# Decay products of a chunked recurrence: another normalization, and their inverses by a backward scan on VectorE

## The chip, the cores and the metric

The kernel runs on one core of one Trainium2 chip. The time is that of one execution on the device, in microseconds (us), as the median of several runs. The profile is that of one further execution of the same program.

## The reference

Three stages follow one another: a linear recurrence over 768 steps for 4 x 8 heads with a state of 40 x 40, an MLP with a leaky ReLU, and a gated MLP behind a root-mean-square norm. The change is in the first.

```python
def _attn_ref(r, k, v, w, a, b):                      # each (4, 8, 768, 40)
    state = np.zeros((B, H, D, D))
    for t in range(S):
        y[:, :, t] = np.einsum('bhd,bhde->bhe', rt, state)
        Sa = np.einsum('bhde,bhe->bhd', state, at)
        state = state * wt[:, :, None, :] - np.einsum('bhd,bhe->bhde', Sa, bt)
        state = state + np.einsum('bhd,bhe->bhde', vt, kt)
...
x = attn_out.transpose(0, 2, 1, 3).reshape(B * S, H * D)   # 3072 x 320
h = x @ w_in; x = np.maximum(0.01 * h, h) @ w_out          # d_ff 2048
xn = x / rms(x) * rms_g
out = (silu(xn @ w_gate) * (xn @ w_val)) @ w_out2          # d_ff 1536
```

The decays `w` lie between 0.85 and 0.95.

## The kernel before

The recurrence is computed in chunks of C = 32 steps, NCH = 24 of them. A chunk has two units (`u = 2c + hs`), each with two batches on the partitions (rows 0 to 39 and 64 to 103 hold the 40 channels) and 8 heads along the free axis, so there are NU = 48 units. Within a chunk the decays enter as running products over time; they are folded into `a`, `k` and `b`, so that the chunk becomes matrix products and a triangular system.

`prep(u)` does this folding, in nine steps that the plan places separately. `scan` (L165): VectorE forms the running products P of one chunk by one `tensor_tensor_scan` over all 8 heads, and the reciprocal of the last product. `ratio` (L170): GpSimd copies the last product (`pc`) and divides all others by it (`pp`). `suffix` (L174): five GpSimd products of shifted slices double the length of products towards the chunk's end, 1, 2, 4, 8, 16, in place in the tile `raw`; they end up as `q`. `ai` (L181) multiplies `a` with `pp`, `kq` (L184) multiplies `k` and `b` with `q` into `kb`, both on GpSimd. `end` (L187): ScalarE squares `pp` and `q` and sums them into `ok`, which a later check reads, and SyncE starts the load of `raw` for the unit after next. For units 0 and 2 (`FAST`) VectorE does GpSimd's part.

Behind it: `stageA` multiplies `kb` with `AI` on TensorE; VectorE masks the result (L238) and ScalarE copies it; over DRAM it is laid out anew for `solve`, in which VectorE solves the triangular systems of a chunk in 31 steps (`tt`, L278, L281 and L283, all with both inputs in SBUF). Stages T, B, C, E and F carry the state through TensorE, with ScalarE and VectorE between them. In `stageF` VectorE makes the next state (`state`, L392, multiplied by `pc` of the following chunk) and the output (`out`, L398, multiplied by `pp`), each with one input in PSUM.

The first MLP runs in between. Its input products (L602) go through ScalarE (L654, L655), VectorE (L654) and GpSimd, which makes the low part `gl` (L655); then come its output products `o` (L610 to L613). Weights are converted and split as jobs `w` (L466 to L480) on VectorE, ScalarE and GpSimd. The second MLP follows when the recurrence is done.

The order is written out by hand: each engine runs its queue in the order in which the program issues. `PROLOG` lists the steps of the first units one by one. From then on each chunk has 12 slots, and `PLAN` gives for even and odd chunks (and some by number) the slot of each step of `prep` for the units three chunks ahead, of the solve's steps, and of the loads and stores. For even chunks the nine steps of the first unit stand in slots 0, 2, 3, 3, 5, 5, 5, 5, 8 and those of the second in 6, 7, 10, 10, 10, 10, 10, 10, 11; for odd chunks in 0, 1, 1, 1, 2, 4, 6, 6, 8 and in 5, 7, 7, 9, 10, 10, 10, 10, 10.

Of the kernel before, what the change touches and what calls it, by code (L numbers as in the profile page):

```python
# [9 lines left out]
F32 = mybir.dt.float32  # L10
# [4 lines left out]
ACTF = mybir.ActivationFunctionType  # L15
ALU = mybir.AluOpType
# [5 lines left out]
C = 32  # L22
NCH = S // C
NU = 2 * NCH
RW = 8 * 34 + 3 * 8 * 32
CW = 32 + 32 + 40 + 32
NT = B * S
DM, DF1, DF2 = 320, 2048, 1536
# [52 lines left out]
class Attn:  # L81
# [3 lines left out]
    def __init__(self, ctx, tc, raw, rT, vS, vT, cst, xs, ok):  # L85
        nc = self.nc = tc.nc
        self.tc = tc
        self.raw_d, self.rT_d, self.vS_d, self.vT_d, self.xs = raw, rT, vS, vT, xs
        per = self.per = ctx.enter_context(tc.tile_pool(name="a_per", bufs=1))
        self.p2 = ctx.enter_context(tc.tile_pool(name="a_p2", bufs=2))  # L90
        self.dr = ctx.enter_context(tc.tile_pool(name="a_dr", bufs=2, space=DRAM))
        self.psp = ctx.enter_context(tc.tile_pool(name="a_ps", bufs=2, space=PSUM))
        self.ends = []
        self.fill = 0
        self.rawt, self.PP, self.PC, self.KBt, self.Nsc, self.Tsc = {}, {}, {}, {}, {}, {}
        self.NT, self.TT, self.tm, self.RHS = {}, {}, {}, {}
        self.load(0)
        self.cst = per.tile([128, CW - 32], F32, name="cst")
        nc.sync.dma_start(out=self.cst, in_=cst[:, 0:CW - 32])
        self.load(1)  # L100
        c = self.cst
        self.mA, self.mE, self.id40 = c[:, 0:32], c[:, 32:64], c[:, 64:104]
        self.d1 = per.tile([128, 272], BF16, name="d1")
        nc.gpsimd.memset(self.d1, 0.0)
        nc.gpsimd.memset(self.d1[:, 0:272:34], 1.0)
        self.ok = ok
        self.AI = per.tile([128, 2, 8, 72], F32, name="ai")
        self.VU = per.tile([128, 2, 8, 64], F32, name="vu")
        self.XZ = per.tile([128, 2, 2, 8, 72], F32, name="xz")
        self.RB = per.tile([128, 2, 2, 8, 40], F32, name="rb")  # L110
        self.G = [per.tile([128, 2, 2, 8, 40], F32, name=f"g{i}") for i in range(3)]
        self.Xa = [per.tile([128, 2, 2, 8, 32], F32, name=f"xa{i}") for i in range(3)]
# [30 lines left out]
    def load(self, u):  # L143
        t = self.p2.tile([128, RW], F32, tag="raw", name="raw")
        self.nc.sync.dma_start(out=t[0:104], in_=self.raw_d[u // 2, u % 2])
        self.rawt[u] = t

    def prep(self, u, fast=False):


        nc = self.nc
        eng = nc.vector if fast else nc.gpsimd
        c, hs = u // 2, u % 2
        raw = self.rawt.pop(u)
        w = raw[0:104, 0:272].rearrange("p (h t) -> p h t", t=34)
        k, b, a = (raw[0:104, 272 + 256 * j:528 + 256 * j].rearrange("p (h t) -> p h t", t=32) for j in range(3))
        q = w[:, :, 2:34]
        P = self.p2.tile([128, 8, 34], F32, tag="P", name="P", bufs=1)
        rp = self.p2.tile([128, 8], F32, tag="rp", name="rp")
        pc = self.p2.tile([128, 8], F32, tag="pc", name="pc", bufs=8)  # L160
        pp = self.p2.tile([128, 8, 32], F32, tag="pp", name="pp", bufs=8)
        kb = self.p2.tile([128, 8, 64], F32, tag="kb", name="kb")
        self.PP[u], self.PC[u], self.KBt[u] = pp, pc, kb

        def scan():  # L165
            nc.vector.tensor_tensor_scan(out=P[0:104].rearrange("p h t -> p (h t)"), data0=raw[0:104, 0:272],  # L166
                                         data1=self.d1[0:104], initial=0.0, op0=ALU.mult, op1=ALU.add)
            nc.vector.reciprocal(rp[0:104], P[0:104, :, 32])

        def ratio():  # L170
            eng.tensor_copy(pc[0:104], P[0:104, :, 32])
            eng.tensor_tensor(pp[0:104], P[0:104, :, 0:32], rp[0:104, :, None].to_broadcast([104, 8, 32]), op=ALU.mult)

        def suffix(*ds):  # L174
            for d in ds:
                eng.tensor_tensor(q[:, :, 0:32 - d], q[:, :, 0:32 - d], q[:, :, d:32], op=ALU.mult)  # L176

        def square(i, x):
            nc.scalar.activation(k, x, ACTF.Square, accum_out=self.ok[0:104, 2 * u + i:2 * u + i + 1])

        def ai():  # L181
            eng.tensor_tensor(self.AI[0:104, hs, :, 0:32], a, pp[0:104], op=ALU.mult)

        def kq(x, o):  # L184
            eng.tensor_tensor(kb[0:104, :, o:o + 32], x, q, op=ALU.mult)

        def end():  # L187
            square(0, pp[0:104])
            square(1, q)
            if u + 2 < NU:  # L190
                self.load(u + 2)

        self.ends.append(end)
        return [scan, ratio, lambda: suffix(1, 2), lambda: suffix(4, 8), lambda: suffix(16), ai,
                lambda: kq(k, 0), lambda: kq(b, 32), end]

    def check(self, flag):

# [172 lines left out]
    def stageF(self, u):  # L371
        nc = self.nc
        c, hs = u // 2, u % 2
        xz, g, rb = self.XZ, self.G[c % 3], self.RB
        last = c == NCH - 1
        n = 32 if last else 72
        ps = self.ps("psF")
        for h in range(8):
            for p in range(2):
                f0, f1 = FR[p]  # L380
                k0, k1 = KF[p]
                nc.tensor.matmul(ps[f0:f1, h // 4, 72 * (h % 4):72 * (h % 4) + n], g[k0:k1, p, hs, h, :], xz[k0:k1, p, hs, h, 0:n],
                                 start=True, stop=True)
        psv = ps[:, :, 0:288].rearrange("p a (h x) -> p a h x", x=72)
        y = self.p2.tile([128, 8, 32], F32, tag="y", name="y")
        pp = self.PP.pop(u)
        self.PC.pop(u)

        def state(p):
            f0, f1 = FR[p]  # L390
            pc = self.PC[u + 2]
            nc.vector.tensor_tensor(rb[f0:f1, p, hs].rearrange("p (a h) d -> p a h d", a=2), psv[f0:f1, :, :, 32:72],  # L392
                                    pc[f0:f1].rearrange("p (a h) -> p a h", a=2)[:, :, :, None].to_broadcast([40, 2, 4, 40]),
                                    op=ALU.mult)

        def out(p):
            f0, f1 = FR[p]
            nc.vector.tensor_tensor(y[f0:f1].rearrange("p (a h) t -> p a h t", a=2), psv[f0:f1, :, :, 0:32],  # L398
                                    pp[f0:f1].rearrange("p (a h) t -> p a h t", a=2), op=ALU.mult)
            b = 2 * p + hs  # L400
            nc.sync.dma_start(out=self.xs[c // 2].rearrange("(h e) (b c t) -> c b e h t", e=40, b=4, c=2)[c % 2, b],
                              in_=y[f0:f1])

        return [lambda f=f, p=p: f(p) for f in ([out] if last else [state, out]) for p in range(2)], []

    def stageT(self, u):
# [467 lines left out]
def run(ctx, tc, nc, raw, rT, vS, vT, cst, w_in, w_out, w_gate, w_val, w_out2, rms_g, out, xs, flag):  # L874
# [37 lines left out]
    def at(g, *fs):  # L912
        todo[g][2].extend(fs)
# [17 lines left out]
    def of(c):  # L931
        return PLAN.get(c, PLAN["odd" if c % 2 else "even"])

    def plan(c):

        g = 12 * c
        P = of(c)
        if c + 3 < NCH:
            for h in range(2):
                parts = {}  # L940
                for n, k in enumerate(P["prep"][h]):
                    at(g + k, lambda n=n, h=h, parts=parts: (parts.setdefault(0, A.prep(2 * c + 6 + h) if not parts else None)[n])())
# [213 lines left out]
def _layouts(r, k, v, w, a, b):  # L1156
    def ft(x):
        return x.reshape(2, 2, H, NCH, C, D).transpose(3, 1, 0, 5, 2, 4)

    def pad(x, fill=0.0):  # L1160
        y = np.full(x.shape[:2] + (104,) + x.shape[4:], fill, np.float32)
        for p in range(2):
            y[:, :, 64 * p:64 * p + D] = x[:, :, p]
        return y

    wp = pad(ft(w), 1.0)
    ws = np.concatenate([np.zeros_like(wp[..., :1]), wp, np.ones_like(wp[..., :1])], -1)
    raw = np.concatenate([x.reshape(NCH, 2, 104, -1) for x in (ws, pad(ft(k)), pad(ft(b)), pad(ft(a)))], -1)
    rT = np.ascontiguousarray(ft(r).transpose(0, 2, 3, 1, 4, 5)).reshape(NCH, 2, D, 512)
    vT = np.ascontiguousarray(pad(ft(v)).transpose(0, 2, 1, 3, 4)).reshape(NCH, 104, 512)  # L1170
    vS = np.ascontiguousarray(v.reshape(2, 2, H, NCH, C, D).transpose(3, 0, 4, 1, 2, 5)).reshape(NCH, 2, C, 640)
    return np.ascontiguousarray(raw), rT, vS, vT
# [26 lines left out]
```

## Time and profile before

| what | value |
|---|---|
| median of 3 runs | 1410.51 us (1409.41 to 1413.34) |
| the profiled execution | 1411.78 us, span 1409.8 us |
| busy: TensorE / VectorE / ScalarE / GpSimd | 1214.3 / 1042.2 / 590.2 / 592.3 us |
| mean granted TensorE clock | 0.900 of full speed |

The span runs from the first to the last instruction. In rows of the profile PE is TensorE (PEld its weight loads), DVE VectorE, ACT ScalarE, POOL GpSimd and SP SyncE. An engine's busy time includes time for which an instruction that has begun is held up. "L283" is line 283 of the kernel; a name before "<-" is the tile written, those behind it are read.

### The profile page before, as it was taken

Reading aid. Unit: us, or ns where it says so; the run is one execution under the profiler, and the core shown is the slowest. Engines: PE = TensorE matmul, PEld = TensorE weight load, DVE = VectorE, ACT = ScalarE, POOL = GpSimd, SP = SyncE. Lnnn points to the kernel's source line nnn. Section 1 sums busy time; section 2 is a strip of 40 time slices with the busy share of each in tenths; the row PEclk is TensorE's granted clock in tenths of the full one; section 3 lists DMA queues with packets and bytes.
Section 4 is the critical chain, followed back from the end, with each engine's and each line's share of the span. In section 5 each row is a group of like instructions: output and inputs, shape, how many; then the busy total and the mean of one; then the engine's idle time right before and its main releaser. Section 6 shows DMA issues by size and latency. Waiting matters only on the chain. (4 is left out here: it accounts for less than half of the span.)

```text
span 1409.8 us, 38871 instructions
## 1 busy us (share of the span) xinstructions
PE 1214.3 (86%) x15609; PEld 1122.0 (80%) x15609; DVE 1042.2 (74%) x2757; ACT 590.2 (42%) x1531; POOL 592.3 (42%) x921
## 2 busy tenths in 40 slices
PE   6677579888788787789878888999999999999996
PEld 4565468777777676778767777898999999999996
DVE  7979999999999999999999988845543333333332
ACT  4335664444434443444443444445633333333332
POOL 6546554545454555544455553223222222222221
PEclk8787588889988989898898989999999999999998
DMA  6536456455536364554544443234200000000000
GB/s 154 129 86 138 122 123 138 117 114 112 120 89 123 96 128 101 109 128 96 120 104 95 88 86 66 56 68 121 68 20 20 20 20 20 20 20 20 21 22 18
DMA packets 243925, 116.90 MB, mean 83 GB/s; under 512 B 194712, under 2 KB 223256, under 8 KB 243736
## 3 DMA queue, kind: packets, MB, share of 16 engines
q1 hardware_dynamic: 223224, 86.14, 28.3%
q10 hardware_dynamic: 20512, 28.19, 7.3%
q8 instruction: 125, 2.05, 0.6%
q14 instruction: 64, 0.52, 0.1%
HBM read 86.36 MB, written 23.99 MB: 78 GB/s over the span
## 5 line engine op out<-in xcount | busy, mean ns | idle before, releaser
L655 POOL TENSOR_TENSOR gl<-t,gh 128x512 fp32r<-128x512 f32 x96 | 131.3, 1368 | 275.9 <-ACT gh L655 274.0
L760 POOL TENSOR_TENSOR gl<-s,gh 128x256 fp32r<-128x256 f32 x144 | 106.4, 739 | 296.2 <-issue 163.2
L757 DVE TENSOR_TENSOR s<-psg,s 128x256 f32<-128x256 f32 x144 | 61.1, 424 | 223.2 <-ACT s L756 222.5
L283 DVE TENSOR_TENSOR tt<-tt,tmp 128x60 f32<-128x60 f32 (+19 forms) x548 | 209.4, 382 | 13.7
L281 DVE TENSOR_TENSOR tmp<-tt,nt 128x60 f32<-128x60 f32 (+19 forms) x548 | 175.3, 320 | 14.4
L176 POOL TENSOR_TENSOR raw<-raw 104x248 f32<-104x248 f32 (+4 forms) x230 | 138.9, 604 | 15.8 <-DVE P L166 2.8
L610 PE MATMUL o<-w1oh,gh 128*128 128x320 f32 x384 | 141.8, 375 | 2.2 <-ACT x L673 2.2
L655 ACT CAST gh<-t 128x512 fp32r<-128x512 f32 x96 | 59.5, 619 | 171.3 <-DVE t L654 163.7
L611 PE MATMUL o<-w1ol,gh 128*128 128x320 f32 x384 | 130.3, 345 | 0.0
L231 PE MATMUL psA<-ai,kb 40*64 40x72 f32 x1536 | 75.8, 263 | 60.6 <-DVE tt L283 24.5
L231 PEld LDWEIGHTS psA<-ai,kb 40*64 40x64 f32 x1536 | 67.9, 166 | 70.4 <-issue 38.9
L602 PE MATMUL psh<-xh,w1ih 128*128 128x256 f32 x384 | 123.4, 342 | 0.5 <-DVE t L654 0.5
L759 ACT CAST gh<-s 128x256 fp32r<-128x256 f32 x144 | 58.5, 406 | 139.2 <-DVE s L758 139.2
L278 DVE SCALAR_TENSOR_TENSOR tt<-nt,tt 128x27 f32<-128x27 f32 (+9 forms) x300 | 109.4, 391 | 4.4 <-DMA nt<-nsc 3.2
L756 ACT ACTIVATE s<-psg 128x256 f32<-128x256 f32 x144 | 55.4, 385 | 115.2 <-PE psg L602 113.4
L602 PE MATMUL psh<-xh,w1il 128*128 128x256 f32 x384 | 103.6, 290 | 0.0
L356 PE MATMUL psE<-xz,vu 40*64 40x72 f32 x1536 | 70.7, 252 | 34.5 <-DVE tt L283 32.8
L613 PE MATMUL o<-w1oh,gl 128*128 128x320 f32 x384 | 97.9, 340 | 0.0
L356 PEld LDWEIGHTS psE<-xz,vu 40*64 40x64 f32 x1536 | 63.2, 156 | 42.6 <-issue 22.3
L610 PEld LDWEIGHTS o<-w1oh,gh 128*128 128x128 f32 x384 | 84.9, 221 | 10.5 <-ACT x L673 2.4
L611 PEld LDWEIGHTS o<-w1ol,gh 128*128 128x128 f32 x384 | 85.7, 223 | 0.0
L602 PEld LDWEIGHTS psh<-xh,w1ih 128*128 128x128 f32 x384 | 76.1, 198 | 12.0 <-DVE t L654 0.8
(171 smaller groups left out, 3551.5 us busy)
## 6 DMA issues: line engine op xcount, KB each, us to landing
raw<-in_raw_dram SPq DMA_DIRECT2D x48, 422.5 KB
nt<-nsc SPq DMA_DIRECT2D x96, 128.0 KB
wst<-in_w_out_dram ACTq DMA_DIRECT2D x23, 256.0 KB
vu<-in_vT_dram SPq DMA_DIRECT2D x24, 208.0 KB
wst<-in_w_in_dram ACTq DMA_DIRECT2D x16, 256.0 KB
xa<-ai SPq DMA_DIRECT2D x48, 80.0 KB
rb<-in_vS_dram SPq DMA_DIRECT2D x48, 80.0 KB
xz<-in_rT_dram SPq DMA_DIRECT2D x48, 80.0 KB
```

The costliest lines, as they stand in the source:

```text
L176: eng.tensor_tensor(q[:, :, 0:32 - d], q[:, :, 0:32 - d], q[:, :, d:32], op=ALU.mult)
L231: nc.tensor.matmul(ps[t0:t1, h // 4, 72 * (h % 4):72 * (h % 4) + 72], kb[f0:f1, h, :], self.AI[f0:f1, hs, h, :], start=True, stop=True)
L278: return [lambda j=j: nc.vector.scalar_tensor_tensor(tt[:, j, s + 1:32], nt[:, s, s + 1:32], tt[:, j, s:s + 1], tt[:, j, s + 1:32], op0=AL ...
L281: return [lambda: nc.vector.tensor_tensor(tmp, tt[:, 0:J, s:s + 1].to_broadcast([128, J, L]), nt[:, s:s + 1, s + 1:32].to_broadcast([128, ...
L283: lambda: nc.vector.tensor_tensor(tt[:, 0:J, s + 1:32], tt[:, 0:J, s + 1:32], tmp, op=ALU.add)]
L356: nc.tensor.matmul(ps[t0:t1, h // 4, 72 * (h % 4):72 * (h % 4) + 72], vu[f0:f1, hs, h, :], xz[f0:f1, p, hs, h, :], start=True, stop=True)
L602: self.nc.tensor.matmul(out, a, x, start=i == 0, stop=i == len(ops) - 1)
L610: mm(out[m], gh[:, sl], h[f], start=first, stop=False)
L611: mm(out[m], gh[:, sl], l[f], start=False, stop=False)
L613: mm(out[m], gl[:, sl], h[f], start=False, stop=last)
L655: [lambda: nc.scalar.copy(gh, t), lambda: nc.gpsimd.tensor_tensor(gl, t, gh.bitcast(F32), op=ALU.subtract)])]
L760: nc.gpsimd.tensor_tensor(gl, s, gh.bitcast(F32), op=ALU.subtract)
```

## The change

The products of a chunk are no longer divided by the last of them: P itself (1 at the chunk's beginning) takes the place of `pp`, and its last column that of `pc`. In place of the suffix products `q` the tile R holds the inverses 1/P. They come from a second `tensor_tensor_scan`, which runs backward over the same decays and in place in `raw`, started in each head by the reciprocal of the head's last product, which the first scan's step puts into a tile `dR` of zeros. So `ratio` becomes `back` on VectorE, the three steps of `suffix` are empty, and the two products for `kb` become one instruction over both. `stageF` multiplies the state by the chunk's own last product. A head's decays take 33 columns in `raw` in place of 34, with one more at the end (1033 columns in all, not 1040). The plan stays as it is; the step at `ratio`'s place is now `back`, and the step at the first `kq`'s place does both products.

```diff
-RW = 8 * 34 + 3 * 8 * 32
+RW = 8 * 33 + 1 + 3 * 8 * 32
...
+        self.dR = per.tile([128, 265], F32, name="dr")
+        nc.gpsimd.memset(self.dR, 0.0)
...
-        P = self.p2.tile([128, 8, 34], F32, tag="P", name="P", bufs=1)
-        rp = self.p2.tile([128, 8], F32, tag="rp", name="rp")
-        pc = self.p2.tile([128, 8], F32, tag="pc", name="pc", bufs=8)
-        pp = self.p2.tile([128, 8, 32], F32, tag="pp", name="pp", bufs=8)
+        P = self.p2.tile([128, 8, 33], F32, tag="P", name="P", bufs=8)
+        R = raw[0:104, 1:265].rearrange("p (h t) -> p h t", t=33)[:, :, 1:33]
...
         def scan():
-            nc.vector.tensor_tensor_scan(out=P[0:104].rearrange("p h t -> p (h t)"), data0=raw[0:104, 0:272],
-                                         data1=self.d1[0:104], initial=0.0, op0=ALU.mult, op1=ALU.add)
-            nc.vector.reciprocal(rp[0:104], P[0:104, :, 32])
-
-        def ratio():
-            eng.tensor_copy(pc[0:104], P[0:104, :, 32])
-            eng.tensor_tensor(pp[0:104], P[0:104, :, 0:32], rp[0:104, :, None].to_broadcast([104, 8, 32]), op=ALU.mult)
-
-        def suffix(*ds):
-            for d in ds:
-                eng.tensor_tensor(q[:, :, 0:32 - d], q[:, :, 0:32 - d], q[:, :, d:32], op=ALU.mult)
+            nc.vector.tensor_tensor_scan(out=P[0:104].rearrange("p h t -> p (h t)"), data0=w[:, 0:264], data1=self.d1[0:104, 0:264],
+                                         initial=0.0, op0=ALU.mult, op1=ALU.add)
+            nc.vector.reciprocal(d[:, 33:265:33], P[0:104, :, 32])
+
+        def back():
+            nc.vector.tensor_tensor_scan(out=w[:, ::-1], data0=w[:, ::-1], data1=d[:, ::-1], initial=0.0,
+                                         op0=ALU.mult, op1=ALU.add)
...
-        def kq(x, o):
-            eng.tensor_tensor(kb[0:104, :, o:o + 32], x, q, op=ALU.mult)
+        def kq():
+            eng.tensor_tensor(kb[0:104].rearrange("p h (j t) -> p j h t", j=2),
+                              raw[0:104, 265:777].rearrange("p (j h t) -> p j h t", j=2, t=32),
+                              R[:, None].to_broadcast([104, 2, 8, 32]), op=ALU.mult)
...
-        return [scan, ratio, lambda: suffix(1, 2), lambda: suffix(4, 8), lambda: suffix(16), ai,
-                lambda: kq(k, 0), lambda: kq(b, 32), end]
+        none = lambda: None
+        return [scan, back, none, none, none, ai, kq, none, end]
...
-            pc = self.PC[u + 2]
...
-                                    pc[f0:f1].rearrange("p (a h) -> p a h", a=2)[:, :, :, None].to_broadcast([40, 2, 4, 40]),
+                                    P[f0:f1, :, 32].rearrange("p (a h) -> p a h", a=2)[:, :, :, None].to_broadcast([40, 2, 4, 40]),
...
-                                    pp[f0:f1].rearrange("p (a h) t -> p a h t", a=2), op=ALU.mult)
+                                    P[f0:f1, :, 0:32].rearrange("p (a h) t -> p a h t", a=2), op=ALU.mult)
```

## Rows read from the trace of the kernel before

**Rows 1.** The page's slices: busy tenths of VectorE, 35 us each.

```profile
DVE  7979999999999999999999988845543333333332
```

**Rows 2.** Stretches: busy us (instructions) of PE, PEld, DVE, ACT, POOL; clock; DMA.

```profile
57.00:865.00 808.00, 648.88 (x10253) 575.70 (x10257) 758.07 (x2047) 357.09 (x953) 415.14 (x672) 0.84 0.50 109
865.00:1000.00 135.00, 127.62 (x1742) 119.54 (x1739) 86.31 (x235) 68.46 (x156) 36.34 (x37) 0.97 0.33 77
```

**Rows 3.** Waits of VectorE, 57 to 865 us: total, times, longest; longest of eight.

```profile
DVE t L654 <- ACT t L654: 3.6, 5, 1.9
DVE tt L278 <- DMA nt<-nsc: 3.2, 1, 3.2
...
```

**Rows 4.** Waits of TensorE, 57 to 865 us, two of them.

```profile
PE psE L356 <- DVE tt L283: 31.2, 15, 5.0
...
PE psC L336 <- ACT rhs L324: 13.0, 5, 9.9
...
```

**Rows 5.** VectorE lines, duration ns min/median/max; L278 to L283 from 57 to 865 us.

```profile
L398 DVE TENSOR_TENSOR y<-psF,pp x96: 406/422/429, 92.0 to 946.6; 40x256 f32<-40x256 f32 x96
...
L278 DVE SCALAR_TENSOR_TENSOR tt<-nt,tt x252: 224/241/1294, 59.3 to 835.9; 128x31 f32<-128x31 f32 x21, 128x29 f32<-128x29 f32 x21, 128x27 f32<-128x27 f32 x21, 128x26 f32<-128x26 f32 x21
...
L281 DVE TENSOR_TENSOR tmp<-tt,nt x484: 148/227/1299, 57.1 to 862.6; 128x60 f32<-128x60 f32 x21, 128x66 f32<-128x66 f32 x14, 128x8 f32<-128x8 f32 x8, 128x63 f32<-128x63 f32 x7
...
L283 DVE TENSOR_TENSOR tt<-tt,tmp x484: 156/226/2523, 57.3 to 862.8; 128x60 f32<-128x60 f32 x21, 128x66 f32<-128x66 f32 x14, 128x8 f32<-128x8 f32 x8, 128x63 f32<-128x63 f32 x7
```

**Rows 6.** Timeline of VectorE in an even chunk: start us, duration us.

```profile
516.24 0.23 DVE L281 TENSOR_TENSOR tmp<-tt,nt 128x66 f32<-128x66 f32 x1
516.50 1.20 DVE L283 TENSOR_TENSOR tt<-tt,tmp 128x66 f32<-128x66 f32 x1
...
518.71 0.49 DVE L281 TENSOR_TENSOR tmp<-tt,nt 128x54 f32<-128x54 f32 x1
...
521.20 0.61 DVE L281 TENSOR_TENSOR tmp<-tt,nt 128x49 f32<-128x49 f32 x1
```

**Rows 7.** Timeline of GpSimd in the same stretch (xN: merged instructions).

```profile
516.34 1.28 POOL L655 TENSOR_TENSOR gl<-t,gh 128x512 fp32r<-128x512 f32 x1 [2.48 <-ACT gh L655]
...
518.55 1.85 POOL L176 TENSOR_TENSOR raw<-raw 104x224 f32<-104x224 f32 x3
...
521.06 1.33 POOL L185 TENSOR_TENSOR kb<-raw 104x256 f32<-104x256 f32 x2
```

**Rows 8.** GpSimd's lines, 57 to 865 us: count, busy us, mean ns, idle before.

```profile
L176 POOL TENSOR_TENSOR raw<-raw 104x192 f32<-104x192 f32 (+4 forms) x215 | 129.4, 602 | 12.2
L655 POOL TENSOR_TENSOR gl<-t,gh 128x512 fp32r<-128x512 f32 x73 | 101.5, 1391 | 185.9 <-ACT gh L655 183.9 <-DMA rb<-in_vS_dram 1.9
L185 POOL TENSOR_TENSOR kb<-raw 104x256 f32<-104x256 f32 x86 | 58.3, 697 | 0.1
L182 POOL TENSOR_TENSOR ai<-raw,pp 104x256 f32<-104x256 f32 x43 | 31.9, 742 | 30.3 <-DMA xa<-ai 27.9 <-PE psA L231 2.3
L172 POOL TENSOR_TENSOR pp<-P,rp 104x256 f32<-104x256 f32 x43 | 30.5, 710 | 0.7
...
L171 POOL COPY pc<-P 104x8 f32<-104x8 f32 x43 | 9.8, 228 | 74.5 <-DVE P L166 74.5
```

**Rows 9.** The solve's lines on VectorE, 57 to 865 us.

```profile
L283 DVE TENSOR_TENSOR tt<-tt,tmp 128x60 f32<-128x60 f32 (+19 forms) x484 | 192.2, 397 | 11.9
L281 DVE TENSOR_TENSOR tmp<-tt,nt 128x60 f32<-128x60 f32 (+19 forms) x484 | 155.2, 321 | 12.5
L278 DVE SCALAR_TENSOR_TENSOR tt<-nt,tt 128x31 f32<-128x31 f32 (+2 forms) x252 | 97.1, 410 | 4.1 <-DMA nt<-nsc 3.2
```

**Rows 10.** VectorE's lines of `prep`, whole span: duration ns min/median/max.

```profile
L166 DVE TENSOR_TENSOR_SCAN P<-raw,d x48: 707/718/727, 5.0 to 848.7; 104x272 f32<-104x272 f32 x48
...
L172 DVE TENSOR_TENSOR pp<-P,rp x2: 424/425/426, 6.0 to 20.5; 104x256 f32<-104x256 f32 x2
...
L176 DVE TENSOR_TENSOR raw<-raw x10: 292/410/686, 8.4 to 22.6; 104x248 f32<-104x248 f32 x2, 104x240 f32<-104x240 f32 x2, 104x224 f32<-104x224 f32 x2, 104x192 f32<-104x192 f32 x2
```

More of the change, by code (lines that the diff above doesn't have):

```diff
@@ L94, in __init__ @@
         self.fill = 0
-        self.rawt, self.PP, self.PC, self.KBt, self.Nsc, self.Tsc = {}, {}, {}, {}, {}, {}
+        self.rawt, self.PP, self.KBt, self.Nsc, self.Tsc = {}, {}, {}, {}, {}
         self.NT, self.TT, self.tm, self.RHS = {}, {}, {}, {}
@@ L104, in __init__ @@
         nc.gpsimd.memset(self.d1, 0.0)
-        nc.gpsimd.memset(self.d1[:, 0:272:34], 1.0)
+        nc.gpsimd.memset(self.d1[:, 0:264:33], 1.0)
+        self.dR = per.tile([128, 265], F32, name="dr")
+        nc.gpsimd.memset(self.dR, 0.0)
         self.ok = ok
@@ L154, in prep @@
         raw = self.rawt.pop(u)
-        w = raw[0:104, 0:272].rearrange("p (h t) -> p h t", t=34)
-        k, b, a = (raw[0:104, 272 + 256 * j:528 + 256 * j].rearrange("p (h t) -> p h t", t=32) for j in range(3))
-        q = w[:, :, 2:34]
-        P = self.p2.tile([128, 8, 34], F32, tag="P", name="P", bufs=1)
-        rp = self.p2.tile([128, 8], F32, tag="rp", name="rp")
-        pc = self.p2.tile([128, 8], F32, tag="pc", name="pc", bufs=8)
-        pp = self.p2.tile([128, 8, 32], F32, tag="pp", name="pp", bufs=8)
+        w = raw[0:104, 0:265]
@@ L162, in prep @@
+        a = raw[0:104, 777:1033].rearrange("p (h t) -> p h t", t=32)
+        P = self.p2.tile([128, 8, 33], F32, tag="P", name="P", bufs=8)
+        R = raw[0:104, 1:265].rearrange("p (h t) -> p h t", t=33)[:, :, 1:33]
         kb = self.p2.tile([128, 8, 64], F32, tag="kb", name="kb")
-        self.PP[u], self.PC[u], self.KBt[u] = pp, pc, kb
+        self.PP[u], self.KBt[u] = P, kb
+        d = self.dR[0:104]
         def scan():
-            nc.vector.tensor_tensor_scan(out=P[0:104].rearrange("p h t -> p (h t)"), data0=raw[0:104, 0:272],
-                                         data1=self.d1[0:104], initial=0.0, op0=ALU.mult, op1=ALU.add)
-            nc.vector.reciprocal(rp[0:104], P[0:104, :, 32])
@@ L178, in square @@
+            nc.vector.reciprocal(d[:, 33:265:33], P[0:104, :, 32])
+        def back():
+            nc.vector.tensor_tensor_scan(out=w[:, ::-1], data0=w[:, ::-1], data1=d[:, ::-1], initial=0.0,
+                                         op0=ALU.mult, op1=ALU.add)
         def square(i, x):
-            nc.scalar.activation(k, x, ACTF.Square, accum_out=self.ok[0:104, 2 * u + i:2 * u + i + 1])
+            nc.scalar.activation(a, x, ACTF.Square, accum_out=self.ok[0:104, 2 * u + i:2 * u + i + 1])
@@ L181, in ai @@
         def ai():
-            eng.tensor_tensor(self.AI[0:104, hs, :, 0:32], a, pp[0:104], op=ALU.mult)
-        def kq(x, o):
-            eng.tensor_tensor(kb[0:104, :, o:o + 32], x, q, op=ALU.mult)
+            eng.tensor_tensor(self.AI[0:104, hs, :, 0:32], a, P[0:104, :, 0:32], op=ALU.mult)
+        def kq():
+            eng.tensor_tensor(kb[0:104].rearrange("p h (j t) -> p j h t", j=2),
+                              raw[0:104, 265:777].rearrange("p (j h t) -> p j h t", j=2, t=32),
+                              R[:, None].to_broadcast([104, 2, 8, 32]), op=ALU.mult)
@@ L187, in end @@
         def end():
-            square(0, pp[0:104])
-            square(1, q)
+            square(0, P[0:104, :, 1:33])
+            square(1, R)
             if u + 2 < NU:
                 self.load(u + 2)
-        self.ends.append(end)
-        return [scan, ratio, lambda: suffix(1, 2), lambda: suffix(4, 8), lambda: suffix(16), ai,
-                lambda: kq(k, 0), lambda: kq(b, 32), end]
+        none = lambda: None
+        return [scan, back, none, none, none, ai, kq, none, end]
     def check(self, flag):
@@ L385, in stageF @@
         y = self.p2.tile([128, 8, 32], F32, tag="y", name="y")
-        pp = self.PP.pop(u)
-        self.PC.pop(u)
+        P = self.PP.pop(u)
         def state(p):
             f0, f1 = FR[p]
-            pc = self.PC[u + 2]
             nc.vector.tensor_tensor(rb[f0:f1, p, hs].rearrange("p (a h) d -> p a h d", a=2), psv[f0:f1, :, :, 32:72],
-                                    pc[f0:f1].rearrange("p (a h) -> p a h", a=2)[:, :, :, None].to_broadcast([40, 2, 4, 40]),
+                                    P[f0:f1, :, 32].rearrange("p (a h) -> p a h", a=2)[:, :, :, None].to_broadcast([40, 2, 4, 40]),
                                     op=ALU.mult)
@@ L1166, in _layouts @@
     wp = pad(ft(w), 1.0)
-    ws = np.concatenate([np.zeros_like(wp[..., :1]), wp, np.ones_like(wp[..., :1])], -1)
+    ws = np.concatenate([np.zeros_like(wp[..., :1]), wp], -1).reshape(NCH, 2, 104, -1)
+    ws = np.concatenate([ws, np.zeros_like(ws[..., :1])], -1)
     raw = np.concatenate([x.reshape(NCH, 2, 104, -1) for x in (ws, pad(ft(k)), pad(ft(b)), pad(ft(a)))], -1)
```

## The prediction

> **What bounds the kernel now.** I read the page's slices first. VectorE shows 9 tenths from the fifth slice to the twenty-fourth and falls off after that [rows 1]. So I cut the span into a stretch of 57 to 865 us, which holds 43 of the 48 preparations [rows 8], and the stretch behind it. In the first VectorE is busy 758 of 808 us, TensorE 649 at a granted clock of 0.84, GpSimd 415 and ScalarE 357; from 865 us TensorE takes over, 128 of 135 us [rows 2]. 94% could still hide waits, so the waits come next: over the 808 us VectorE waited for anything named for some 12 us in all, 3.6 at most for one pair [rows 3], and the other 38 us of idle time spread over 2047 instructions, 18 ns each. TensorE's longest waits are for VectorE's solve (`tt`) [rows 4]. VectorE is therefore the bound of these 808 us: a microsecond that it gains or loses there moves the end by about as much, since the work behind 865 us stays the same.
>
> The question then is what VectorE's microseconds are made of. A product with one input in PSUM, L398, takes 406 to 429 ns in all 96 cases. The solve's instructions, which read SBUF twice, have medians of 226 to 241 ns but reach 1.3 to 2.5 us [rows 5]. The timelines of both engines say why. A 128x66 product takes 0.23 us at 516.24. The next one of that size, at 516.50, takes 1.20 and ends at 517.70; GpSimd's L655 ran from 516.34 to 517.62. The one at 518.71 ends at 519.20, as the first of three L176 does (1.85/3 = 0.62 from 518.55, so 519.17). The one at 521.20 ends at 521.81, where the first of two L185 is done (521.06 plus 0.67) [rows 6, 7]. A VectorE instruction with two SBUF inputs that meets a GpSimd one ends just after it. VectorE's busy time contains time blocked by GpSimd, and the steps taken from GpSimd count on VectorE's side.
>
> **The change, part by part.**
>
> *Blocking that goes.* In the 808 us the solve's blocked time is busy time less count times undisturbed duration. With medians: 192.2 - 484 x 0.226 = 82.8, 155.2 - 484 x 0.227 = 45.3, 97.1 - 252 x 0.241 = 36.4, together 164; the medians hold some blocking themselves, so this is low. With the minima (0.156, 0.148, 0.224), which belong to the smallest shapes and so are too low: 116.7 + 83.6 + 40.7 = 241. I take the middle, 203 [rows 5, 9]. GpSimd's removed steps are L176 129.4, L172 30.5 and L171 9.8, or 169.7 of its 415 us, 41% [rows 2, 8]. Blocking shared out by busy time gives 0.41 x 203 = **-83 us** (67 to 99). The weight conversions on VectorE are lengthened too; I leave them out.
>
> *Two preparations that were VectorE's own.* Units 0 and 2 did ratio and doubling on VectorE: 10 x 0.410 + 2 x 0.424 = 5.0 us [rows 10]. **-5**, all ahead of 57 us, where the first solve waits for that chain.
>
> *The backward scan.* 48 more on VectorE. The row before has no reversed scan, and none in place. The nearest is the forward one, 0.718 us for 272 elements, so 0.70 for 265; with the 18 ns behind each instruction 48 x 0.72 = **+34.6**. Below, it can't be cheaper than a product of 256, 0.42 (+21); above, I find no row, and put twice the forward scan (+69). The row of the same operation decides for 0.70. The forward scan drops 8 elements: 48 x 8/272 x 0.718 = **-1**.
>
> *The fused product on GpSimd* (`kq`): two of 0.697 become one of 512 elements, for which L655 shows 1.39: the same time [rows 8]. But two left a gap through which one VectorE instruction of 0.23 could pass. Between 0 and 48 x 0.23 = 11, I take **+3**: only preparations that meet a dense solve lose it.
>
> *The new scan's own blocking.* It reads two SBUF tiles, and GpSimd no longer stands still for it. The forward scan was never lengthened, 707 to 727 ns in 48 cases [rows 10], yet GpSimd's next step often waited for just that scan (75 us before L171 [rows 8]), so this is weak evidence. Between 0 and the rival's 33 below I take **+3**.
>
> *At nothing.* The `state` product has the same shape with the multiplier in another tile, filled long before. The squares on ScalarE have the same size and ScalarE idles more than half of the stretch [rows 2]; without that cover they would cost nothing new either. The reciprocal only writes elsewhere. No DMA is moved: the load of `raw` keeps its last step behind the squares, on SyncE, and shrinks by 7 of 1040 elements. One wait is new: the fused product waits for the backward scan, and behind it on GpSimd stands `gl`, for which TensorE's `o` products wait. The plan puts the backward scan three or more slots ahead of the product in the steady chunks, and a slot is 808/(21.5 x 12) = 3.1 us, so it is done in time. Where GpSimd's stalls end sooner, its next wait is one for ScalarE or a DMA and off the path.
>
> Sum: -83 - 5 - 1 + 34.6 + 3 + 3 = -48. VectorE now waits 12 us for others; being quicker it will meet a few more late inputs, for which I give back 3: **-45**. The profiled execution took 1411.8 us for a span of 1409.8, 1.3 above the median of 1410.5, so the forecast on the median's scale is **1365**.
>
> [...]
>
> **The rivals.**
>
> *The backward scan is caught.* If each of the 48 starts behind a GpSimd instruction and waits half of L655's 1.39, that is +33 in place of +3: -15, 1395. For it: the two solve lines are caught this way. Against it: GpSimd is left with 415 - 170 = 245 of some 760 us, so a third of the scans should meet anything. 0.10.
>
> *Another engine comes last.* TensorE is at 80% of the stretch and each chunk's state goes through TensorE, VectorE and ScalarE in turn; if half of the gain turns into waits, 1388. For it: some of TensorE's waits are for ScalarE [rows 4]. Against it: those of VectorE are 12 us in 808 [rows 3], and the wanted gain is 6% of the stretch. 0.11.
>
> *The blocking only moves.* GpSimd's remaining work is the same and VectorE's solve as dense; if half of the 83 returns behind `gl` and the fused product, -45 + 41 = -4, 1407: no change that shows. Against it: the 245 us left are met at the same rate, about 0.49 us of blocking each, as now. 0.06.
>
> *The reversed in-place scan is slow.* The other side. The change breaks even when one takes 0.70 + 45/48 = 1.64 us; at three times the forward row, 2.1 us, the sum is 48 x 1.4 - 45 = +22, 1432. For it: no row has a negative step or an output over its own input. Against it: the forward row is steady to 20 ns. 0.05.
>
> **How the numbers follow.** 0.68 for the forecast. Its own range, from 67 to 99 us of blocking and up to 8 more for the fused product, is 1345 to 1385. The first two rivals lie at 1388 and 1395, so up to 1392 the range holds about 8 in 10; below, the blocking of the weight conversions that I left out stays within 1345. Faster by more than 0.3% (4 us, about what a measurement can tell): 0.68 + 0.10 + 0.11 = 0.89; within: 0.06; slower: 0.05.
>
> **What would show it.** In the profile after: a second scan line on VectorE, 48 of about 0.70 us; the means of L283 and L281 (397 and 321 ns now) down by a fifth; GpSimd's busy time in the stretch down by some 170 us; VectorE still above 90% up to the end of the attention, which then ends some 45 us sooner, and TensorE's part behind it unchanged. The prediction is wrong if the backward scan takes over 1.6 us or spreads by more than 0.3 us, if L655 and the fused product block so much that L283's mean stays, or if VectorE shows tens of microseconds of waits for ScalarE, TensorE or a DMA.

## The result, and the profile after

The changed kernel takes 1351.06 us (1348.42 to 1355.24, 4 runs) where the kernel before took 1409.96 beside it; the ratio is 0.9581, with a 95% interval of 0.955 to 0.9611. That is 59 us less. The profiled execution is the shortest of the four: 1348.42 us, span 1346.6, against 1409.8 before.

The page's slices, then two stretches, with the columns of [rows 2]. The last preparation's squares on ScalarE end at 866.0 us before and at 805.3 us now, so the first stretch is given up to 811 and up to 805.3 us.

```profile
DVE  6979999999999999999999898555533333333332
```
```profile
57.00:811.00 754.00, 622.74 (x10362) 549.43 (x10363) 705.69 (x2106) 356.28 (x954) 242.88 (x327) 0.89 0.55 117
57.00:805.30 748.30, 617.72 (x10275) 544.90 (x10276) 700.38 (x2086) 354.00 (x947) 241.68 (x326) 0.89 0.55 117
811.00:946.00 135.00, 127.54 (x1684) 119.27 (x1683) 85.26 (x226) 71.64 (x158) 37.39 (x40) 1.00 0.34 83
```

The stretch that took 809 us up to 866.0 takes 748 for the same work (10275 instructions on TensorE, 10278 before). Up to 811 us, for which the views below are given, it is 754 and holds some 90 of them more. VectorE is busy 706 of the 754, 94% as before [rows 2]; GpSimd fell from 415 to 243. What stands behind is unchanged: from the start of the last output product to the end of the span it is 461.8 us, and it was 463.2. The granted clock changes within the stretch (1.00 from 65 to 74 us, 0.50 from 75 to 81); its mean rose from 0.84 to 0.89, and TensorE's busy share from 80% to 83%. That can have given little: VectorE waited for TensorE 1.4 us in the whole stretch before, and 2.3 now.

VectorE's named waits in the stretch, the longest of seven:

```profile
DVE tt L275 <- DMA nt<-nsc: 3.3, 1, 3.3
DVE xa L235 <- ACT g L240: 2.5, 4, 1.3
...
```

They come to 10.5 us, against 12.4 before [rows 3]. So VectorE is still the bound, and the difference lies in its busy time. The solve's lines in the stretch (L278 and L280 were L281 and L283, L275 was L278), and then the two scans and the output product over the whole span with min/median/max in ns:

```profile
L278 DVE TENSOR_TENSOR tmp<-tt,nt 128x60 f32<-128x60 f32 (+19 forms) x483 | 149.7, 310 | 12.5
L280 DVE TENSOR_TENSOR tt<-tt,tmp 128x60 f32<-128x60 f32 (+19 forms) x483 | 145.5, 301 | 11.9
L275 DVE SCALAR_TENSOR_TENSOR tt<-nt,tt 128x27 f32<-128x27 f32 (+7 forms) x263 | 77.0, 317 | 4.4 <-DMA nt<-nsc 3.3
```
```profile
L166 DVE TENSOR_TENSOR_SCAN P<-raw,d x48: 693/702/728, 5.3 to 791.0; 104x264 f32<-104x264 f32 x48
...
L171 DVE TENSOR_TENSOR_SCAN raw<-raw,dr x48: 695/702/1780, 6.2 to 794.8; 104x265 f32<-104x265 f32 x48
...
L393 DVE TENSOR_TENSOR y<-psF,P x96: 406/422/429, 83.7 to 884.8; 40x256 f32<-40x256 f32 x96
```

The solve takes 372 us in place of 444.5 [rows 9], for nearly the same work: the means of its three lines went from 397, 321 and 410 to 301, 310 and 317 ns. The new scan costs 0.702 us in the median. The last output product starts at 884.8 us, 61.8 earlier than the 946.6 of [rows 5]; the first one at 83.7, so 8.3 of that were won ahead of it.

GpSimd's lines in the stretch:

```profile
L650 POOL TENSOR_TENSOR gl<-t,gh 128x512 fp32r<-128x512 f32 x74 | 101.3, 1369 | 322.7 <-ACT gh L650 322.7
L181 POOL TENSOR_TENSOR kb<-raw 104x512 f32<-104x512 f32 x43 | 51.4, 1195 | 2.6 <-DVE raw L171 2.6
L178 POOL TENSOR_TENSOR ai<-raw,P 104x256 f32<-104x256 f32 x42 | 30.8, 732 | 48.1 <-DMA xa<-ai 33.3 <-PE psC L333 12.2 <-PE psA L228 1.2
```

The fused product takes 1.19 us, less than the 1.39 that the two of before took together [rows 8]. The wait that the change adds, for the backward scan, is 2.6 us in all.

### The profile page after: what moved, and what is told of

Same layout as the page of the kernel before. It is cut to its first block, busy times and chain, and to the rows that moved or that the text cites. A ratio compares the mean times of both kernels' runs of the same rounds, so it can differ in the third digit from the quotient of the medians.

```text
span 1346.6 us, 38515 instructions
## 1 busy us (share of the span) xinstructions
PE 1176.7 (87%) x15609; PEld 1086.3 (81%) x15609; DVE 980.3 (73%) x2789; ACT 587.7 (44%) x1531; POOL 408.3 (30%) x554
## 5 line engine op out<-in xcount | busy, mean ns | idle before, releaser
L278 DVE TENSOR_TENSOR tmp<-tt,nt 128x60 f32<-128x60 f32 (+19 forms) x548 | 168.4, 307 | 14.4
L280 DVE TENSOR_TENSOR tt<-tt,tmp 128x60 f32<-128x60 f32 (+19 forms) x548 | 161.6, 295 | 13.7
L605 PE MATMUL o<-w1oh,gh 128*128 128x320 f32 x384 | 132.6, 352 | 2.3 <-ACT x L668 2.3
L606 PE MATMUL o<-w1ol,gh 128*128 128x320 f32 x384 | 122.5, 326 | 0.0
L353 PE MATMUL psE<-xz,vu 40*64 40x72 f32 x1536 | 70.7, 252 | 56.8 <-DVE xa L235 23.5
L275 DVE SCALAR_TENSOR_TENSOR tt<-nt,tt 128x27 f32<-128x27 f32 (+9 forms) x300 | 85.3, 311 | 4.7 <-DMA nt<-nsc 3.5
L605 PEld LDWEIGHTS o<-w1oh,gh 128*128 128x128 f32 x384 | 78.1, 203 | 9.6 <-ACT x L668 2.5
L228 PE MATMUL psA<-ai,kb 40*64 40x72 f32 x1536 | 61.7, 233 | 23.3 <-ACT vu L338 7.4
L228 PEld LDWEIGHTS psA<-ai,kb 40*64 40x64 f32 x1536 | 54.5, 139 | 32.7 <-ACT vu L338 8.6
L597 PE MATMUL psh<-xl,w1ih 128*128 128x256 f32 x384 | 78.8, 288 | 0.0
L606 PEld LDWEIGHTS o<-w1ol,gh 128*128 128x128 f32 x384 | 78.6, 205 | 0.0
```

The costliest lines, as they stand in the source:

```text
L228: nc.tensor.matmul(ps[t0:t1, h // 4, 72 * (h % 4):72 * (h % 4) + 72], kb[f0:f1, h, :], self.AI[f0:f1, hs, h, :], start=True, stop=True)
L275: return [lambda j=j: nc.vector.scalar_tensor_tensor(tt[:, j, s + 1:32], nt[:, s, s + 1:32], tt[:, j, s:s + 1], tt[:, j, s + 1:32], op0=AL ...
L278: return [lambda: nc.vector.tensor_tensor(tmp, tt[:, 0:J, s:s + 1].to_broadcast([128, J, L]), nt[:, s:s + 1, s + 1:32].to_broadcast([128, ...
L280: lambda: nc.vector.tensor_tensor(tt[:, 0:J, s + 1:32], tt[:, 0:J, s + 1:32], tmp, op=ALU.add)]
L353: nc.tensor.matmul(ps[t0:t1, h // 4, 72 * (h % 4):72 * (h % 4) + 72], vu[f0:f1, hs, h, :], xz[f0:f1, p, hs, h, :], start=True, stop=True)
L597: self.nc.tensor.matmul(out, a, x, start=i == 0, stop=i == len(ops) - 1)
```

## The experiments

The theory is the prediction's: GpSimd's instructions block VectorE's (a 128x66 product took 1.20 us in place of 0.23 [rows 6, 7]), VectorE is the bound, so lifting them shortens the run by the time blocked, less what the scan costs. The expectations put it down to their reading of SBUF; those rows don't show that, and e2 tests it. The first rival is the chain: the preparation is shorter, so `kb` reaches TensorE sooner. The second is GpSimd's occupancy. VectorE's busy time and the span are those of each profiled run.

| run | median us | ratio to before, interval | VectorE busy us | span us |
|---|---|---|---|---|
| before | 1409.7 to 1411.1 | 1 | 1042.2 | 1409.8 |
| after | 1351.06 | 0.9581 (0.955 to 0.9611) | 980.3 | 1346.6 |
| e1_steps_back | 1422.57 | 1.008 (1.0058 to 1.0102) | 1054.7 | 1420.5 |
| e2_writes_only | 1359.28 | 0.9644 (0.9623 to 0.9664) | 983.6 | 1355.6 |
| e3_no_scan | 1343.15 | 0.9525 (0.9507 to 0.9543) | 959.3 | 1340.1 |
| e4_two_products | 1350.59 | 0.958 (0.9555 to 0.9605) | 975.2 | 1346.2 |
| e5_product_on_vector | 1343.24 | 0.9519 (0.9497 to 0.954) | 973.5 | 1341.4 |
| e6_one_scan_more | 1389.34 | 0.984 (0.9819 to 0.9861) | 1012.8 | 1390.2 |
| e7_scan_alone | 1440.3 | 1.0208 (1.0192 to 1.0223) | 1072.5 | 1436.5 |
| e8_vector_no_scan | 1325.96 | 0.9388 (0.9351 to 0.9426) | 945.1 | 1325.4 |
| e9_copy_for_scan | 1349.28 | 0.9568 (0.9536 to 0.96) | 960.0 | 1347.3 |

### GpSimd's steps put back

```diff
 # after
+        k = raw[0:104, 265:521].rearrange("p (h t) -> p h t", t=32)
+        def ones(*ds):
+            for d in ds if not fast else ():
+                nc.gpsimd.tensor_tensor(k[:, :, 0:32 - d], k[:, :, 0:32 - d],
+                                        P[0:104, :, 0:1].to_broadcast([104, 8, 32 - d]), op=ALU.mult)
-        return [scan, back, none, none, none, ai, kq, none, end]
+        return [scan, lambda: (back(), ones(0)), lambda: ones(1, 2), lambda: ones(4, 8), lambda: ones(16), ai, kq, none, end]
```

> The changed kernel with six GpSimd products put back at the places of ratio and suffix: k times the first column of P, which is 1, in the old shapes; the output stays the reference's. Blocking (the gain is time for which VectorE's two-input instructions no longer wait for GpSimd): some 165 us of SBUF-reading work on GpSimd return, at about 0.49 us of blocking each, so +80, 1415 to 1445, above the kernel before, since the backward scan stays; the solve's lines lengthen again. Chain (the gain comes from kb being ready sooner for TensorE): the products stand ahead of kb again, so at most the whole gain of 59 is lost, 1410 or less, and the solve's lines stay short.

It took 1422.57 us, 71.5 more than the changed kernel. Over the whole span, the products put back and the solve:

```profile
L195 POOL TENSOR_TENSOR raw<-raw,P 104x256 f32<-104x256 f32 (+5 forms) x276 | 173.0, 627 | 104.3 <-DVE P L166 82.2 <-ACT wab L467 4.8 <-DVE dr L168 1.8
...
L287 DVE TENSOR_TENSOR tt<-tt,tmp 128x60 f32<-128x60 f32 (+19 forms) x548 | 196.6, 359 | 13.7
L285 DVE TENSOR_TENSOR tmp<-tt,nt 128x60 f32<-128x60 f32 (+19 forms) x548 | 172.9, 316 | 14.4
L282 DVE SCALAR_TENSOR_TENSOR tt<-nt,tt 128x27 f32<-128x27 f32 (+9 forms) x300 | 111.4, 397 | 4.5 <-DMA nt<-nsc 3.2
```

173 us of GpSimd work that nothing needs lengthened the solve from 415 to 481 us over the whole span (161.6 + 168.4 + 85.3 in the changed kernel) and VectorE in all by 74, and the span by 74. The run lies above the kernel before, which the chain can't give. A microsecond of such work cost 0.41 of the run.

### The same time on GpSimd, but only writing

```diff
 # before
             for d in ds:
-                eng.tensor_tensor(q[:, :, 0:32 - d], q[:, :, 0:32 - d], q[:, :, d:32], op=ALU.mult)
+                for _ in range(2): nc.gpsimd.memset(q[:, :, 0:32 - d], 1.0)     # GpSimd's units
```

> The kernel before, with each of GpSimd's five doubling products replaced by two memsets of the same slice (about the same time on GpSimd, but it only writes); q is then all ones, so the decays towards a chunk's end are left out of the output. Blocking by reads of SBUF: the 60 us that L176 blocks go, 1340 to 1360. GpSimd's occupancy or the chain behind it: the steps take as long as before, so no change, 1405 to 1415.

It took 1359.28 us, 52 less than the kernel before.

```profile
L177 POOL MEMSET raw<- 104x248 f32 (+4 forms) x460 | 127.6, 278 | 25.5 <-DVE P L166 2.7
...
L286 DVE TENSOR_TENSOR tt<-tt,tmp 128x60 f32<-128x60 f32 (+19 forms) x548 | 182.5, 333 | 13.7
L284 DVE TENSOR_TENSOR tmp<-tt,nt 128x60 f32<-128x60 f32 (+19 forms) x548 | 164.9, 301 | 14.4
L281 DVE SCALAR_TENSOR_TENSOR tt<-nt,tt 128x27 f32<-128x27 f32 (+9 forms) x300 | 83.4, 304 | 5.7 <-DMA nt<-nsc 4.4
```

GpSimd worked 128 us in place of 139 in these steps and in the same order ahead of `kb`; its whole busy time hardly changed (579 us against 592). The solve fell from 494 to 431 us all the same. The timelines show it beside the memsets, at 0.23 us an instruction:

```profile
505.99 2.71 POOL L177 MEMSET raw<- 104x248 f32 x8
```
```profile
507.06 0.23 DVE L284 TENSOR_TENSOR tmp<-tt,nt 128x69 f32<-128x69 f32 x1
507.32 0.23 DVE L286 TENSOR_TENSOR tt<-tt,tmp 128x69 f32<-128x69 f32 x1
507.59 0.23 DVE L284 TENSOR_TENSOR tmp<-tt,nt 128x66 f32<-128x66 f32 x1
507.85 0.23 DVE L286 TENSOR_TENSOR tt<-tt,tmp 128x66 f32<-128x66 f32 x1
```

A rival is left: a memset is half as long as a product, so it could hold VectorE just as often and only for a shorter time. The trace settles it. Of the 213 solve instructions that began beside a product L176 in the kernel before, 71% took over 0.1 us more than the median of their line and shape with GpSimd idle, 54 us in all. Of the 325 that began beside a memset here, 1% did, 5 us in all. So for the solve it is the products, which read SBUF, that block, and not the memsets, which only write: occupancy and chain are both out. The run gained less than the solve because the norm's L678, which multiplies 320 columns by one number per row, rose from 9.9 to 17.9 us beside memsets and `gl` (last section).

### What a scan costs

```diff
 # e7, from before, and e6, from after: the forward scan twice
         def scan():
+          for _ in range(2):
             nc.vector.tensor_tensor_scan(out=P[0:104].rearrange("p h t -> p (h t)"),
...
 # e3, from after: no backward scan
-        return [scan, back, none, none, none, ai, kq, none, end]
+        return [scan, none, none, none, none, ai, kq, none, end]
```

> The kernel before with the forward scan of each unit done twice, the same result: the change's cost on VectorE alone. VectorE is the bound there by its waits: 48 x 0.74 = +35, 1440 to 1450. If part of a scan fits into time in which VectorE would wait or be blocked anyway: less, 1420 to 1435.

> The changed kernel with the forward scan of each unit done twice, the same result. If VectorE is still the one bound: 48 x 0.72 = +35, 1380 to 1392. If the changed kernel has come to where others end last as well, as the run without the backward scan suggests (8 us for 36): +10 to +25.

> The changed kernel without the backward scan; k and b are then multiplied by the decays themselves, which leaves the inverses out of the output. VectorE is the bound: 48 scans of 0.75 us go, -36, 1312 to 1322. The scan is hidden behind waits of VectorE: no change, 1347 to 1355.

A scan more cost 29.4 us in the kernel before (48 x 0.61) and 38.3 in the changed one (48 x 0.80), both as expected for VectorE as the bound, the first at the lower end of its range. A scan less gave only 7.9, for 36.1 us of scans on VectorE. Two things took the rest. VectorE's total fell by 21 us, not 36, because other lines took longer: the first step of the weight conversion rose from 29.5 us to 42.3 and the forward scan from 33.7 to 38.0, while the solve took 7 less. Without the scan 13 of the 85 conversions begin some 40 ns behind the start of a fused product and are held to its end; with the scan 13 begin in a product's last 7 ns and take 0.28 us. The timelines of VectorE and GpSimd in e3, and that line:

```profile
334.45 1.29 DVE L461 TENSOR_SCALAR wf<-wst 128x256 uint32<-128x256 uint32 x1
```
```profile
334.41 1.18 POOL L181 TENSOR_TENSOR kb<-raw 104x512 f32<-104x512 f32 x1
```
```profile
L461 DVE TENSOR_SCALAR wf<-wst 128x256 uint32<-128x256 uint32 x85 | 42.3, 498 | 0.3
```

And VectorE's idle time (span less busy) rose from 366 to 381 us; of its named waits from 57 to 780 us, 23.5 in all, the two longest are

```profile
DVE t L649 <- ACT t L649: 8.2, 11, 1.2
DVE rb L387 <- PE psF L379: 5.2, 7, 2.1
...
```

against 0.2 and 2.3 in the changed kernel. So two explanations stood: from about 1343 us down others come last as often as VectorE (a knee), or the plan's slots happened to line up badly without the scan. Two runs were to tell them apart.

```diff
 # e9, from after: a small copy at the scan's place
-            nc.vector.tensor_tensor_scan(out=w[:, ::-1], data0=w[:, ::-1], data1=d[:, ::-1], initial=0.0,
-                                         op0=ALU.mult, op1=ALU.add)
+            nc.vector.tensor_copy(w[:, 33:265:33], d[:, 33:265:33])
 # e8, from e5 (below): no backward scan
-        return [scan, back, none, none, none, ai, kq, none, end]
+        return [scan, none, none, none, none, ai, kq, none, end]
```

> The changed kernel with the backward scan replaced by a VectorE copy of the 8 reciprocals into the same tile, so that the fused product still waits for VectorE at the scan's place; the inverses are left out of the output but for each head's last. The copy takes about 0.15 us. Knee: 1338 to 1347, as without any scan. Alignment: -27, 1320 to 1328.

> The changed kernel with the fused product for kb on VectorE and without the backward scan; k and b are multiplied by the decays themselves, so the inverses are left out of the output. Knee (below some 1343 others end last as well): 1335 to 1343, with VectorE waiting longer for ScalarE and TensorE. Alignment (without the scan the fused product on GpSimd met VectorE's conversions, which can't happen with it on VectorE): VectorE's 36 us come off, 1305 to 1315.

Neither theory came through. With the copy the run took 1349.28 us, so nothing is won by giving the product something to wait for (a copy took 0.226 us in the mean, the scan 0.752); but that is also above the knee's range, and the conversion is blocked again:

```profile
L460 DVE TENSOR_SCALAR wf<-wst 128x256 uint32<-128x256 uint32 x85 | 41.7, 491 | 0.3
```

With the product on VectorE the scan's absence gave 17 us (1343.24 to 1325.96): well below the supposed knee, but only half of 36, although VectorE's busy time fell by 28. Idle time was 387 us in e9, 380 in e8 and 377 in e6, which has more work for VectorE, not less; it was 364 to 372 in the seven others. So there is no floor at 1343, and it isn't only work that sets the idle time. That taking an instruction out of a chunk, or putting one in, shifts what the plan lines up, for some 10 to 20 us, is the likely cause but not shown; only the conversion behind the fused product is known as such a pair, in e3 and e9.

### The fused product

```diff
 # e4, from after: two products on GpSimd
-        def kq():
-            eng.tensor_tensor(kb[0:104].rearrange("p h (j t) -> p j h t", j=2),
-                              raw[0:104, 265:777].rearrange("p (j h t) -> p j h t", j=2, t=32),
-                              R[:, None].to_broadcast([104, 2, 8, 32]), op=ALU.mult)
+        def kq(j):
+            eng.tensor_tensor(kb[0:104, :, 32 * j:32 * j + 32],
+                              raw[0:104, 265 + 256 * j:521 + 256 * j].rearrange("p (h t) -> p h t", t=32), R, op=ALU.mult)
...
-        return [scan, back, none, none, none, ai, kq, none, end]
+        return [scan, back, none, none, none, ai, lambda: kq(0), lambda: kq(1), end]
 # e5, from after: the fused product on VectorE
-            eng.tensor_tensor(kb[0:104].rearrange("p h (j t) -> p j h t", j=2),
+            nc.vector.tensor_tensor(kb[0:104].rearrange("p h (j t) -> p j h t", j=2),
```

> The changed kernel with the fused product for kb split into the two of before, one behind the other on GpSimd. By the prediction's step (a gap between two lets one VectorE instruction through): 3 us faster, up to 10, 1341 to 1349. By GpSimd's busy time (the fused one took 1.19, the two 1.39 us): 46 x 0.2 x 0.5 = 5 us slower, 1356.

1350.59 us against 1351.06: no difference that can be measured, and neither of the two expectations. GpSimd took 8 us more for the two. The solve took 7 us less and the conversion's first step 6 more (35.8 against 29.5), so what the gap gives in one place is lost in another.

> The changed kernel with the fused product for kb on VectorE for all units. On VectorE it costs 46 x 0.70 = 32 us; on GpSimd it blocked VectorE for about 41 us by the trace of the changed kernel. Blocking that goes with the work: -9, 1338 to 1347. Blocking that only moves to the rest of GpSimd's work: +32 in place of it, 1375 to 1385.

1343.24 us, 8 less than the changed kernel, and 0.9519 of the kernel before: the best version here with the whole computation. Its interval and the changed kernel's just fail to overlap (0.9497 to 0.954, 0.955 to 0.9611).

```profile
L280 DVE TENSOR_TENSOR tt<-tt,tmp 128x60 f32<-128x60 f32 (+19 forms) x548 | 153.6, 280 | 13.7
L278 DVE TENSOR_TENSOR tmp<-tt,nt 128x60 f32<-128x60 f32 (+19 forms) x548 | 144.9, 264 | 14.3
...
L181 DVE TENSOR_TENSOR kb<-raw 104x512 f32<-104x512 f32 x48 | 33.3, 694 | 0.1
L461 DVE TENSOR_SCALAR wf<-wst 128x256 uint32<-128x256 uint32 x85 | 25.3, 298 | 0.3
```

VectorE does 33.3 us of products itself (1.8 of them were its own already), and the solve's first two lines take 31.5 us less, the conversion's first step 4 less: on GpSimd the product had blocked VectorE for more than VectorE needs to do it.

## Why the prediction was right

The direction, the mechanism and the time came out inside the range of 1345 to 1392, 14 us below the 1365 forecast and 6 us above the range's lower end. (From its own bounds, 67 to 99 us of blocking and 0 to 11 for the fused product, the forecast's own range comes out as 1346 to 1389, not 1345 to 1385.) By its steps:

- **VectorE is the bound, at one to one.** It held for the change itself (62 us less of work, 63 less of span) and, within 5 us, for e1, e2 and e7. It is not a law of this kernel: e3, e6, e8 and e9 have 11 to 21 us more of idle time than the kernels they were made from.
- **Blocking that goes, -83.** With the +3 for the fused product, which shows in the solve's lines too, the forecast for the solve was -80. It measured 444.5 to 372.2 us in the stretch, -72, and 494.1 to 415.3 over the whole span, -79. e1 and e2 show that it is blocking, by reads. The trace also lets the blocked time be counted, as what each solve instruction took above the median of its line and shape with GpSimd idle. In the 808 us that is 184 us, 79 of them in instructions that began beside the removed L176, L172 or L171; in the changed kernel's 754 us it is 111. So sharing it out by busy time was right, and the 203, taken as the middle between 164 and 241, was a guess that came out close: that part is luck.
- **What was left out.** The prediction did not count the other VectorE lines that GpSimd holds up. They give 9 us, more than half of them in the norm's small instructions. Two of these over the whole span, in the kernel before and in the changed one (count, busy us, mean ns):

```profile
L680 DVE TENSOR_TENSOR q<-q,v 128x2 f32<-128x2 f32 x12 | 4.8, 400 | 0.1
L681 DVE TENSOR_SCALAR r<-r 128x2 f32<-128x2 f32 x12 | 4.7, 392 | 0.1
```
```profile
L676 DVE TENSOR_SCALAR r<-r 128x2 f32<-128x2 f32 x12 | 2.0, 163 | 0.1
L675 DVE TENSOR_TENSOR q<-q,v 128x2 f32<-128x2 f32 x12 | 1.9, 155 | 0.1
```

  An instruction on two columns that takes 400 ns in the mean was blocked time in plain sight: 7 of the 12 were held beside a GpSimd product before, none after. This is the main term that was mis-sized: 0, where 9 was right.
- **The scan, +34.6.** 48 of 0.752 are 36.1 us. In place and backward it costs what the forward one does, 0.702 us in the median. An element of it takes about twice as long as one of a product, by an estimate that takes the 155 ns of a product of two columns (L675 above) off as a fixed cost: 2.06 ns (702 ns for 265) against 1.04 (422 for a product of 256).
- **The rival that the scan is caught.** It happens, but seldom: 4 of the 48 began beside a GpSimd instruction that reads and took 0.74 to 1.78 us, 17 began beside a memset and took 0.70 to 0.71. In all 36.1 less 48 x 0.702 is 2.4 us, near the +3 put down for it and far from 33. By its letter this is one of the signs of being wrong that the prediction named (a spread of more than 0.3 us); it weighs little because so few were caught.
- **Two preparations of VectorE's own, -5**, and **the fused product, +3.** The first were 6 us in the trace, and the first output product of the recurrence comes 8.3 us sooner. The second was nothing (e4).
- **The 3 us given back for waits** were not needed: named waits fell by 2.
- **A sign that failed.** The means of both L283 and L281 were to fall by a fifth. L283's fell by 24% and L281's by only 3%; the rest of the gain came in the solve's third line, L278, 410 to 317 ns.

Together: -79 for the solve, -9 for the lines left out, -6 for the own preparations, +36 for the scan and -1 for the shorter forward one are -59, and the medians differ by 59. That they agree to the microsecond is chance: records of neighbouring instructions overlap (VectorE's lines in the kernel before come to 1113.5 us one by one, its busy time to 1042.2), and VectorE's busy time fell by 62 and the span by 63 in the profiled runs. Against the forecast 9 of the missing 14 us are the lines left out, 3 the waits; the rest is spread over small terms.

## What to carry to other kernels

The busy time of an engine that is the bound can hold another engine's work, as VectorE's did here (184 us of the solve's 444.5 in the stretch before): compare the median and the maximum of one shape, and find the maximum's end in the other engine's timeline. Then price a step on the second engine by what it blocks, here 0.4 to 0.5 us for each microsecond (0.41 of the run in e1, 0.46 of the solve in e2), against what it would cost on the first; a serial scan of 0.7 us beat six elementwise steps of 0.6. In a schedule that is written out by hand, allow for idle time that an edit may add, whatever its sum says: here 11 to 21 us, in e3, e6, e8 and e9.

## What the runs showed of the hardware that was not expected

An instruction of VectorE with a single SBUF tile as input can be blocked too: L461 takes 0.28 us for 256 columns of 32 bits in the median, quicker than a product's 0.42, and rose to 1.29 behind the fused product in e3. Instructions of the norm with a single input were held by memsets as well, which left the solve alone. Two of its lines in e2, with min/median/max in ns:

```profile
L684 DVE TENSOR_SCALAR r<-r x12: 151/308/317, 252.6 to 947.4; 128x2 f32<-128x2 f32 x12
L678 DVE TENSOR_SCALAR x<-x,q x24: 375/532/1684, 253.9 to 948.1; 128x320 f32<-128x320 f32 x24
```

Seven of the twelve L684 began 20 ns behind the start of a memset and took 308 to 317 ns, to just behind its end; the four that met nothing took 162 to 170. So in e2 memsets held these and not the solve's instructions, which have two SBUF inputs. Not every single input is held either: the reciprocal L168 took 205 to 208 ns in all 48 cases of the changed kernel, four of them beside a GpSimd instruction that reads. The output product with one input in PSUM never was, 406 to 429 ns in both kernels, with 17 of its 96 beside such an instruction.

GpSimd's product of 104x512 with one factor broadcast took 1.19 us, where one of 128x512 with two full inputs, and an output of another type, took 1.37.
